# Softmax attention and linear attention on one core: the overflow guard moves from maxima of queries and keys to the row sums, and normalization and value copies move from VectorE to GpSimd

## The chip, the core and the metric

The kernel runs on one core of a Trainium2 chip. A core has a matrix engine (TensorE, "PE" in the profile), a vector engine (VectorE, "DVE"), an engine for activation functions (ScalarE, "ACT"), a general engine (GpSimd, "POOL") and a queue that issues transfers (SyncE, "SP"). PE writes its products into PSUM, eight banks of 128 x 512 float32; the others read PSUM or SBUF, and here POOL works on SBUF alone. The metric is the time of one execution on the device in microseconds (us).

## The reference

Two blocks of the same sizes are computed and set side by side in the output: A is linear attention, B is softmax attention. Each has its own input x (2048 x 512) and weights.

```python
B, S, D = 1, 2048, 512;  H = 32; Dh = 16
qkv = (x @ wqkv) -> q, k, v of (B, H, S, Dh)
# A: linear attention
phi = lambda t: jnp.where(t > 0, t + 1, jnp.exp(t)) + 1e-6
kv = jnp.einsum("bhsd,bhse->bhde", phi(k), v);  z = sum over s of phi(k)
o = (phi(q) @ kv) / (phi(q) @ z + 1e-6);  a = o @ wo
# B: softmax attention
p = softmax((q @ k.T) * Dh ** -0.5);  o = p @ v;  b = o @ wo
return jnp.concatenate([a, b], axis=-1)      # (1, 2048, 1024)
```

Almost all of the work is the 32 x 2048 x 2048 exponentials of block B.

## The kernel before

**Blocks and units.** The scores of B are made transposed, keys along the partitions, in blocks of 128 keys x 512 queries of one head: 32 heads x 4 query chunks x 16 key tiles = 2048 blocks. Heads are taken in four groups of eight (`Gp`). A unit (`unit(u)`, 32 of them) is one group, one chunk of 512 queries and either the even or the odd heads of the group: 4 heads x 16 key tiles = 64 blocks, whose products with the values accumulate in one PSUM bank `PVb`. The values `VV` have 17 columns for a head, the last of them ones, so that column 16 of the sum is the row sum of the softmax.

**Two ways to an exponential.** A block goes one of two ways. On the ACT way (`fill_act_cand`, L1022) ACT reads two or three score blocks from the PSUM regions `pS` and writes exp of them to `PT` in float16; each block then needs one product with the values. On the D way (`d_emit`, L923) a block lands in a bank of `pD` (or in the last bank of `pS`, which is "lent"), and DVE turns the scores into the bit patterns of float16 numbers with one multiply-and-add into int16 (`DI`): a straight line through the exponent. Three patterns shifted by a third of an octave each, weighted, approximate exp more closely; so up to three blocks of `DI` (1536 columns) are shifted twice (`shift_cand`, L1093) into `DJ`, on POOL as a rule, and PE multiplies `DI` and both `DJ` with three copies of the values, `VV` with k = 0, 1, 2, the last two weighted by `SW`. A D block costs ACT nothing, DVE one pass, POOL two shifts and PE three products.

**The other jobs.** `proj_job` projects queries and keys, copies them out of PSUM on DVE (L557, L563, L571) and then takes the largest absolute value of each 512 columns (L558 into `QMX`, L565 and L584 into `KMX`). `bound_job` (L595 to L601) and `flag_job` (L606, L607) turn these maxima into a bound on every score and leave the largest in `FLG`. `v4_job` projects four tiles of values: DVE copies them out of PSUM (L625) and makes the two weighted copies (L629), 32 of these in all. When a unit's sum is complete, `unit_done` transposes it on DVE into `OT` (L1241), takes reciprocals of the row sums (L1252), normalizes into `XN`, a part of the tile `OT` (L1246), and after each second unit transposes back into `ON` (L1256) for the output projection; `last_unit_done` (L1181 to L1189) does the last unit in halves. Block A's jobs (`akv_job` and the following ones) are spread over the run.

**What sets the order.** The program is planned when it is built: a loop keeps a clock for each engine, takes the candidate that can start first (ties by priority) and writes the instruction down. Each engine then runs its list in that order, with semaphore waits where data pass between engines. The durations in the code (0.62 for a reduction, `dp` and `dd` for a shift, the factors `PACE`) are the planner's, and are not measurements. How many blocks go the D way is no constant: `d_pick` (L869) gives a block to the D way whenever a bank is free, the planned backlog of DVE is at most `DBL` and that of POOL (`p_backlog`, L858) at most `PBL`, and a `DI` buffer is free. `shift_cand` gives a shift to DVE instead of POOL when POOL would end it more than `LM` = 5 us later.

**The guard.** A second, general program (`_general_softmax`) follows, for inputs whose scores could overflow the patterns. Every engine loads `FLG` into a register (L1480), 200 entries of the plan behind the instruction that writes it, and branches to the general program at its end only if the flag is above the threshold.

```python
d_pick:  if bi is None or u is None or dfree[bi] > at or d_backlog(at) > DBL or p_backlog(at) > PBL or lagging(at): return None
shift_cand:  dp, dd = 0.157 + w * 0.00095, 0.22 + w * 0.00047
             ln, st_, d_ = ("dve", sd, dd) if tp > td + LM else ("pool", sp, dp)
unit_done:   mul = f_op("dve", lambda e: e.tensor_tensor(xn[:, :, 16 * e_:16 * e_ + 16], o[:, :, 0:16], zr..., op=ALU.mult)
```

## Time and profile before

| What | Value |
|---|---|
| Runs, median (lowest to highest) | 701.72 us (701.65 to 701.93), 3 runs |
| Profiled execution, its own time | 701.74 us |
| Its span, first to last instruction | 700.0 us |
| Around the span | 1.74 us |
| Mean granted clock of PE | 0.999 |
| Busy: PE, DVE, ACT, POOL | 660.2, 619.5, 681.3, 577.1 us |

The profile is of one execution. "L923 DVE TENSOR_SCALAR DI<-pD 128x512 ... x431 | 285.5, 679 | 31.5 <-PE pD L821 26.5" reads: line 923 of the program, on DVE, writes DI from pD; 431 instructions that were busy for 285.5 us together, 679 ns each on average; ahead of them the engine sat idle for 31.5 us, of which 26.5 ended with a result of PE from line 821. Instructions of one engine overlap somewhat, so the busy time of a group can be less than its count times its mean. In a view of windows each row is a stretch of time and the columns are the busy time of each engine, with the number of its instructions. In a view of waits a row names who waited, for whom, how long in all, how often, and the longest. In a timeline a row begins with the start and the duration in us; the view of one line's instructions gives the shortest, median and longest duration in ns.

### The profile page before, as it was taken

To read this page: it belongs to the slowest core of one execution; us is meant where nothing else is said; L and a number is where in the kernel's file an instruction comes from. 1 tells how busy PE (TensorE), PEld (TensorE's weight loads), DVE (VectorE), ACT (ScalarE), POOL (GpSimd) and SP (SyncE) were. 2 spreads that over 40 slices of the span, in tenths; PEclk is the share of its full clock that TensorE was granted. 3 is DMA by queue.
4 is the path that set the end of the run, shared out by engine and by line. 5 is a ranking of instruction groups with operands and counts; after the bars stand their busy time and mean duration, and the time that the engine had idled before them with its cause. 6 is when DMAs were issued, how large, how long until landed. Compare 5 with 4: busy or idle time off the path is not lost.

```text
span 700.0 us, 19238 instructions
## 1 busy us (share of the span) xinstructions
PE 660.2 (94%) x8355; PEld 210.6 (30%) x8355; DVE 619.5 (88%) x994; ACT 681.3 (97%) x703; POOL 577.1 (82%) x409
## 2 busy tenths in 40 slices
PE   7999989999999999999999999999999999999996
PEld 4323333333333333332232233232322222322222
DVE  5999998898797989979998999999889999879993
ACT  5999999999999999999999999999999999999995
POOL 5689977776998889969967998889698898779983
PEclk9999999999999999999999999999999999999999
DMA  9300002211011000310012101110201100011001
GB/s 204 98 3 2 16 17 22 42 24 38 3 24 25 16 18 16 70 35 11 8 37 38 32 1 25 28 51 17 39 9 31 31 10 16 17 47 31 24 31 35
DMA packets 55418, 21.75 MB, mean 31 GB/s; under 512 B 45600, under 2 KB 55328, under 8 KB 55328
## 3 DMA queue, kind: packets, MB, share of 16 engines
q1 hardware_dynamic: 54272, 20.20, 13.2%
q8 instruction: 67, 1.10, 0.7%
q10 hardware_dynamic: 1056, 0.26, 0.2%
q14 instruction: 23, 0.19, 0.1%
HBM read 4.19 MB, written 4.19 MB: 12 GB/s over the span
## 4 chain that ended last, share of the span: by engine, by line
ACT 74%; DVE 16%; PE 7%; SPq 1%; issue 1%; DMA 1%; ACTq 0%
ACT PT L1022 71%; DVE DI L923 8%; PE pS L821 3%; PE pPV L1141 2%; ACT pD L641 2%; DVE VV L629 2%; DVE OT L1246 2%; PE pD L520 1%; SPq L371 1%; DVE VV L625 1%; DMA Wb<-in_B_wqkv_dram 1%; DVE OT L1241 1%; DVE KV L524 0%; PE pD L821 0%; DVE KV L640 0%
## 5 line engine op out<-in xcount | busy, mean ns | idle before, releaser
L1022 ACT ACTIVATE PT<-pS 128x1024 f16<-128x1024 f32 (+1 forms) x665 | 670.3, 1297 | 3.9 <-PE pS L821 1.6
L1093 POOL TENSOR_SCALAR DJ<-DI 128x1536 int16<-128x1536 int16 x384 | 569.7, 1485 | 110.3 <-DVE DI L923 86.5
L923 DVE TENSOR_SCALAR DI<-pD 128x512 int16<-128x512 f32 (+1 forms) x439 | 295.2, 689 | 32.0 <-PE pD L821 26.7
L821 PE MATMUL pS<-QT,KM 32*128 32x512 bf16 x1601 | 261.8, 384 | 24.2 <-ACT PT L1022 17.0
L1141 PE MATMUL pPV<-PT,VV 128*17 128x512 f16 x1446 | 244.1, 382 | 0.4 <-DVE VV L625 0.4
L1141 PE MATMUL pPV<-DJ,VV 128*17 128x512 f16 x1204 | 229.2, 382 | 0.4 <-DVE VV L629 0.4
L821 PE MATMUL pD<-QT,KM 32*128 32x512 bf16 x447 | 161.9, 384 | 1.9 <-DVE KV L524 0.9
L821 PEld LDWEIGHTS pS<-QT,KM 32*128 32x128 bf16 x1601 | 64.8, 91 | 274.4 <-ACT PT L1022 239.8
L1141 PE MATMUL pPV<-DI,VV 128*17 128x512 f16 x602 | 145.6, 382 | 0.3 <-DVE OT L1241 0.2
L923 DVE TENSOR_SCALAR DI<-pS 128x512 int16<-128x512 f32 x155 | 105.0, 678 | 4.2 <-PE pS L821 2.7
L1141 PEld LDWEIGHTS pPV<-PT,VV 128*17 128x17 bf16 x1446 | 50.2, 88 | 51.8 <-issue 44.8
L1141 PEld LDWEIGHTS pPV<-DJ,VV 128*17 128x17 bf16 x1204 | 48.0, 88 | 44.5 <-issue 33.8
L821 PEld LDWEIGHTS pD<-QT,KM 32*128 32x128 bf16 x447 | 38.4, 91 | 17.1 <-DVE DI L923 7.5
L1141 PEld LDWEIGHTS pPV<-DI,VV 128*17 128x17 bf16 x602 | 30.9, 88 | 20.8 <-issue 16.5
L520 PE MATMUL pD<-Wa,xTa 128*32 128x256 bf16 x896 | 34.6, 275 | 1.3 <-DVE DI L923 1.0
L1246 DVE TENSOR_TENSOR OT<-OT,ZR 128x256 bf16<-128x256 f32 x31 | 34.2, 1102 | 0.2
L520 PE MATMUL pD<-xTb,Wb 128*32 128x512 bf16 x400 | 29.4, 383 | 0.8 <-DVE DI L923 0.5
L629 DVE TENSOR_SCALAR VV<-VV 128x544 bf16<-128x544 bf16 x32 | 24.8, 789 | 0.0
L641 ACT ACTIVATE pD<-pD 128x512 f32<-128x512 f32 x30 | 23.6, 786 | 0.8 <-DVE KV L640 0.7
L520 PEld LDWEIGHTS pD<-Wa,xTa 128*32 128x32 bf16 x896 | 19.7, 96 | 14.4 <-issue 7.9
L1241 DVE STREAM_TRANSPOSE OT<-pPV 128x512 f32<-128x512 f32 x31 | 21.9, 707 | 0.4 <-PE pPV L1141 0.2
L520 PE MATMUL pD<-xTa,Wa 128*32 128x256 bf16 x512 | 19.8, 275 | 0.1
(98 smaller groups left out, 359.3 us busy)
## 6 DMA issues: line engine op xcount, KB each, us to landing
out_dram<-KV SPq DMA_DIRECT2D x32, 128.0 KB, 1.7
Wa<-in_A_wqkv_dram SPq DMA_DIRECT2D x3, 512.0 KB, 4.5
KM<-KR SPq DMA_DIRECT2D x96, 16.0 KB, 1.8
Wb<-in_B_wqkv_dram SPq DMA_DIRECT2D x2, 384.0 KB, 4.3
Wb<-in_B_wqkv_dram SPq DMA_DIRECT2D x1, 512.0 KB, 4.4
Wa<-in_A_wo_dram SPq DMA_DIRECT2D x1, 512.0 KB, 4.2
Wb<-in_B_wo_dram SPq DMA_DIRECT2D x1, 512.0 KB, 3.7
xTa<-in_A_x_dram SPq DMA_TRANSPOSE x24, 3.4
```

The lines of the kernel that those rows point to most:

```text
L371: sch.add(lane, lambda e: e.dma_start_transpose(dst[:, :, t0 * 128:(t0 + n) * 128], x[0][t0 * 128:(t0 + n) * 128, :]), writes=[(dname, t) ...
L520: ins = e.matmul(out[32 * g:32 * g + 32], lhsT=lhsT[:, 32 * g:32 * g + 32], rhs=rhs, start=start, stop=stop, tile_position=(0, 32 * g))
L625: st.append(("dve", 0.6, f_ev("dve", lambda e, bk: e.tensor_copy(VV[:, sl, 0, 4 * t4:4 * t4 + 4, :].rearrange("p t (h c) -> p t h c", c=17 ...
L629: st.append((lane, 0.4 if lane == "dve" else 0.71, f_op(lane, lambda e, k=k: e.tensor_scalar(vv(k), vv(0), SW[k], 0.0, op0=ALU.mult, op1=A ...
L641: ex = lambda bk: sch.add("act", lambda e: e.activation(x(bk), x(bk), ACTF.Exp), reads=[bk[3]], writes=[bk[3]])
L821: return e.matmul(dst, lhsT=KM[32 * g:32 * g + 32, Gp % 2, e_, j * 128:(j + 1) * 128], rhs=QT[32 * g:32 * g + 32, Gp % 2, c * 512:(c + 1) ...
L923: sch.add("dve", lambda e: e.tensor_scalar(DI[:, buf, i * 512:(i + n) * 512], f32v(DBANK[bi], 512 * n), ESC, EB, op0=ALU.mult, op1=ALU.add ...
L1022: sch.add("act", lambda e: e.activation(PT[:, row, c0:c0 + w], SCR[sl][:, 0:w], ACTF.Exp, scale=SC), reads=skeys(sl)[:len(bl)], writes=[(" ...
L1093: sch.add(ln, lambda e: e.tensor_scalar(J, I, 1.0, float(SH[k]), op0=ALU.mult, op1=ALU.add), reads=[("DI", buf, i) for i in range(n)], wri ...
L1141: sch.add("pe", lambda e, g=g, j=j, h=h, k=k, P=P, first=first, last_=last_: e.matmul(PVb[32 * g:32 * g + 17, 0:512], lhsT=VV[:, Gp % 2, k ...
L1241: sch.add("dve", lambda e: e.transpose(OT[:, 0, :], PVb[:, 0:512]), reads=[("PV", g) for g in range(4)], writes=[("OT", 0)])
L1246: mul = f_op("dve", lambda e: e.tensor_tensor(xn[:, :, 16 * e_:16 * e_ + 16], o[:, :, 0:16], zr.unsqueeze(2).broadcast_to([128, 16, 16]), ...
```

## The change

1. *The guard.* The maxima of queries and keys go (L558, L565, L584), and so does the bound made of them. The reciprocals of the row sums of all units, which were overwritten from unit to unit, are kept in `ZRA`. `sums_job` takes their largest and smallest when unit 30 is done (two reductions over 496 columns), `bound_job` adds the last unit's 16 columns and compares with 1/512 and 1/60000, `flag_job` brings the result to one number by a matmul into `PVb` and a reduction on DVE. These jobs are in a new list, `late`, with the lowest priority. PE, ACT, DVE and SP load the flag at the end of their lists, POOL behind its wait for the last stores.
2. *Clamped unsigned patterns.* Keys are stored multiplied by `ESC`, so the D way's first step is now an addition of `EB` and a minimum with `IMAX` into uint16; ACT's scale is divided by `ESC`.
3. *Normalization* of units 0 to 30 is issued on POOL (`XNP` = 1); `OT` and `XN` have one buffer each. *The weighted copies of the values* of groups 1 to 3 (24 of 32) are issued on POOL; those of group 0 stay on DVE.
4. *The planner.* POOL's planned shift becomes `POOLT(w)` = 0.284 + 0.00082 w with `PACE` 1.0 (before 0.157 + 0.00095 w with 1.01); a shift on DVE 0.40 + 0.0003 w (before 0.22 + 0.00047 w); `p_backlog` counts waiting shifts at `POOLT`; `PBL` goes from 6.5 to 7.5 and `SEED`, which jitters the due times of block A's jobs, from 14 to 18. On POOL a normalization has the priority 0.5, a shift 0.7 and a value copy 2 (the smaller goes first).
5. *Setting up.* The float32 identity, which only the general program uses, is no longer made at the start.

```diff
-    PBL = 6.5
+    PBL = 7.5
-    SEED = 14
+    SEED = 18
-    PACE = {"pe": 1.0, "act": 1.0, "dve": 1.03, "pool": 1.01, "dma": 1.0}
+    XNP = 1
+    VVP = 0
+    POOLT = lambda w: 0.284 + w * 0.00082
+    PACE = {"pe": 1.0, "act": 1.0, "dve": 1.03, "pool": 1.0, "dma": 1.0}
+    IMAX = 31743.0 - SH[2]
+    RMIN, RMAX = 512.0, 60000.0
...
-        OT = sb("OT", [128, 2, 512], F32)
-        XN = OT.bitcast(BF)[:, 1, :].rearrange("p (x n) -> p x n", n=512)
-        ZR = sb("ZR", [128, 2, 16], F32)
+        OT = sb("OT", [128, 1, 512], F32)
+        XN = sb("XN", [128, 1, 512], BF)
-        mk_ident(identf, "identf")
...
 proj_job
-                st.append(("dve", 0.62, f_op("dve", lambda e: e.tensor_reduce(QMX[:, i:i + 1], QT[:, r, cs], axis=AX.X, op=ALU.max,
-                                                                             apply_absolute_value=True), [("QT", r, sc)], [("QMX", i)])))
-                st.append(("dve", 1.2, f_op("dve", lambda e: e.tensor_reduce(KMX[:, i:i + 1], KM[:, r, :, cs], axis=AX.XY, op=ALU.max,
-            st.append(("dve", 0.62, reduce))
-            cp = f_ev("dve", lambda e, bk: e.tensor_copy(KR[:, kr, :], f32v(bk)), [], [("KR", kr)])
+            cp = f_ev("dve", lambda e, bk: e.tensor_scalar(KR[:, kr, :], f32v(bk), ESC, None, op0=ALU.mult), [], [("KR", kr)])
...
+        def red(dst, lo, hi, op):
+            return lambda e: e.tensor_reduce(ZRA[:, dst:dst + 1], ZRA[:, lo:hi], axis=AX.X, op=op)
+        ZL = 16 * (NU - 1)
+        def sums_job(**kw):
+            return Job([("dve", 0.6, f_op("dve", red(ZL + 16, 0, ZL, ALU.max), [("ZR", u) for u in range(NU - 1)], ["ZMX"])),
+                        ("dve", 0.6, f_op("dve", red(ZL - 1, 0, ZL, ALU.min), [("ZR", u) for u in range(NU - 1)], [("ZR", NU - 2)]))],
+                       [("zr", NU - 2)], [(1, "sums")], bank=False, **kw)
         def bound_job(**kw):
+                ("dve", 0.15, f_op("dve", red(ZL + 16, ZL, ZL + 17, ALU.max), ...
+                ("dve", 0.15, f_op("dve", red(ZL - 1, ZL - 1, ZL + 16, ALU.min), ...
+                ("dve", 0.12, f_op("dve", lambda e: e.tensor_scalar(BN1[:], ZRA[:, ZL + 16:ZL + 17], 1.0 / RMIN, None, op0=ALU.is_gt), ["ZMX"], ["BN1"])),
+                ("dve", 0.12, f_op("dve", lambda e: e.scalar_tensor_tensor(BN1[:], ZRA[:, ZL - 1:ZL], 1.0 / RMAX, BN1[:], op0=ALU.is_lt, op1=ALU.add),
         def flag_job(**kw):
+                ("pe", 0.3, f_op("pe", lambda e: e.matmul(PVb[0:1, 0:128], lhsT=BN1[:], rhs=BMk[:], start=True, stop=True), ["BN1", "BMk"], pvk)),
+                ("dve", 0.3, f_op("dve", lambda e: e.tensor_reduce(FLG, PVb[0:1, 0:128], axis=AX.X, op=ALU.max), pvk, ["FLG"]))],
...
-        def v4_job(t4, Gp, lane="dve", **kw):
+        def v4_job(t4, Gp, lane="pool", **kw):
-                st.append((lane, 0.4 if lane == "dve" else 0.71, f_op(lane, lambda e, k=k: e.tensor_scalar(
+                st.append((lane, 0.74 if lane == "dve" else 0.73, f_op(lane, lambda e, k=k: e.tensor_scalar(
...
 p_backlog
-            w += 1.13 * len(pend)
+            w += sum(POOLT(p_[3]) for p_ in pend)
-                    w += 1.13 * len(s_["items"])
+                    w += 2 * POOLT(512 * DG) / DG * len(s_["items"])
 d_emit
-                    sch.add("dve", lambda e: e.tensor_scalar(DI[:, buf, i * 512:(i + n) * 512], f32v(DBANK[bi], 512 * n),
-                                                             ESC, EB, op0=ALU.mult, op1=ALU.add),
+                    sch.add("dve", lambda e: e.tensor_scalar(DI.bitcast(U16)[:, buf, i * 512:(i + n) * 512], f32v(DBANK[bi], 512 * n),
+                                                             EB, IMAX, op0=ALU.add, op1=ALU.min),
 shift_cand
-            dp, dd = 0.157 + w * 0.00095, 0.22 + w * 0.00047
+            dp, dd = POOLT(w), 0.40 + w * 0.0003
-            return st_, 0, ln, d_, run, None, "f"
+            return st_, 0.7 if ln == "pool" else 0, ln, d_, run, None, "f"
...
 unit_done
-            mul = f_op("dve", lambda e: e.tensor_tensor(xn[:, :, 16 * e_:16 * e_ + 16], o[:, :, 0:16],
+            mul = f_op("pool" if XNP else "dve", lambda e: e.tensor_tensor(xn[:, :, 16 * e_:16 * e_ + 16], o[:, :, 0:16],
-                  ("dve", 0.68, norm)]
+                  ("pool", 0.82, norm) if XNP else ("dve", 0.96, norm)]
...
-        bjobs.append(bound_job(ready=0))
-        bjobs.append(flag_job(ready=0))
+        late = [sums_job(ready=0), bound_job(ready=0), flag_job(ready=0)]
...
-            sch.emit_queue(queue, e, sems, hook=(flag_op.idx + 200, hook))
-            with e.If(got[0] > THRESHOLD_BITS):
+            sch.emit_queue(queue, e, sems, hook=(flag_op.idx if queue == "pool" else len(sch.ops), hook))
+            with e.If(got[0] > FLAG_BITS):
```

More of the change, by code (lines that the diff above doesn't have):

```diff
@@ L135, in _general_softmax @@
     MBb = MB.bitcast(BF)
+    sch.add("dve", lambda e: e.memset(PVb[:], 0.0), writes=["PV"])
+    sch.add("pool", lambda e: e.memset(identf[:], 0.0), writes=["identf"])
+    sch.add("pool", lambda e: e.affine_select(out=identf[:], in_=identf[:], compare_op=ALU.not_equal, fill=1.0,
+                                              base=0, pattern=[[-1, 128]], channel_multiplier=1), reads=["identf"], writes=["identf"], force_signal=True)
     for Gp in range(4):
@@ L177, in _general_softmax @@
             sch.add("dve", lambda e: e.tensor_scalar(GM[:, 0, :], GM[:, 0, :], -1.0, None, op0=ALU.mult), reads=["GM"], writes=["GM"])
-            sch.add("pe", lambda e: e.transpose(MB[0:NT, 0:128], GM[:, 0, :], identf[:]), reads=["GM"], writes=["MB"])
+            sch.add("pe", lambda e: e.transpose(MB[0:NT, 0:128], GM[:, 0, :], identf[:]), reads=["GM", "identf"], writes=["MB"])
             sch.add("dve", lambda e: e.tensor_copy(GT, MB[0:NT, 0:128]), reads=["MB"], writes=["GT"])
@@ L331, in bass_concat_heads__linear_attn_block__softmax_full_mha__prompt_kernel @@
         PAR = sb("PAR", [128, 2], F32)
-        QMX = sb("QMX", [128, NGP * NC], F32)
-        KMX = sb("KMX", [128, NGP * NC], F32)
-        BND = sb("BND", [128, NGP], F32)
+        ZRA = sb("ZRA", [128, 16 * NU + 1], F32)
         BN1 = sb("BN1", [128, 1], F32)
-        FLG = sb("FLG", [1, 1], F32)
         NS, NA = len(ABL), sum(ABL)
@@ L407, in bass_concat_heads__linear_attn_block__softmax_full_mha__prompt_kernel @@
         mk_ident(identb, "identb")
[L408 to L409 removed]
+        sch.add("dve", lambda e: e.memset(DUM, 0.0), writes=["FLG"])
+        sch.add("act", lambda e: e.activation(DUM[:, 4:8], DUM[:, 0:4], ACTF.Exp), reads=["FLG"], writes=["FLG"])
         sch.add("dve", lambda e: e.memset(FZ[:], 0.0), writes=["FZ"])
@@ L604, in flag_job @@
         def flag_job(**kw):
+            pvk = [("PV", g) for g in range(4)]
             return Job([
-                ("pe", 0.3, f_pe(lambda e, bk: e.matmul(bk[0][0:1, bk[2]:bk[2] + 128], lhsT=BN1[:], rhs=BMk[:], start=True, stop=True), ["BN1", "BMk"])),
-                ("dve", 0.3, f_ev("dve", lambda e, bk: e.tensor_reduce(FLG[:], bk[0][0:1, bk[2]:bk[2] + 128], axis=AX.X, op=ALU.max), [], ["FLG"]))],
-                ["BN1"], [], **kw)
+                ("pe", 0.3, f_op("pe", lambda e: e.matmul(PVb[0:1, 0:128], lhsT=BN1[:], rhs=BMk[:], start=True, stop=True), ["BN1", "BMk"], pvk)),
+                ("dve", 0.3, f_op("dve", lambda e: e.tensor_reduce(FLG, PVb[0:1, 0:128], axis=AX.X, op=ALU.max), pvk, ["FLG"]))],
+                ["BN1"], [], bank=False, **kw)
@@ L632, in v4_job @@
             needs = ["WbV"] + [("xTb", t) for t in ts] + ([("pvdone", Gp - 2)] if Gp >= 2 else [])
-            return Job(st, needs, [(k, ("V", Gp, t, k)) for k in range(3) for t in ts], rel=0, **kw)
+            return Job(st, needs, [(k, ("V", Gp, t, k)) for k in range(3) for t in ts], rel=2 if VVP == 1 and lane == "dve" else 0, **kw)
         ectr = [0]
@@ L1291, in bass_concat_heads__linear_attn_block__softmax_full_mha__prompt_kernel @@
         urgent, urgent2, early, bjobs, ajobs = [], [], [], [], []
-        urgent2.append(Job([kmx], gives=[(0, ("KMX", 0))], bank=False, ready=30.0))
-        urgent2.append(Job([qmx], gives=[(0, ("QMX", 0))], bank=False, ready=30.0))
         for sc in range(1, NC):
@@ L1335, in job_cand @@
             bi = min((i for i in range(ND + 1) if dfree[i] is not None), key=lambda i: dfree[i], default=None)
-            for lst, pr in ((urgent, 0.5), (early, 2), (bjobs, 2.2), (urgent2, 2.3), (ajobs, 2.5)):
+            for lst, pr in ((urgent, 0.5), (early, 2), (bjobs, 2.2), (urgent2, 2.3), (ajobs, 2.5), (late, 2.7)):
                 for pos, j_ in enumerate(lst[:1] if lst is not urgent2 else lst[:8]):
@@ L1449, in bass_concat_heads__linear_attn_block__softmax_full_mha__prompt_kernel @@
                 TRACE.append((st, st + dur, eng, o[1]))
-        assert all(l_ == 0 for l_ in left) and pvu[0] == NU and not (urgent or urgent2 or early or bjobs or ajobs), \
+        assert all(l_ == 0 for l_ in left) and pvu[0] == NU and not (urgent or urgent2 or early or bjobs or ajobs or late), \
             (left, pvu, len(urgent), len(urgent2), len(early), len(bjobs), len(ajobs))
```

87 lines of the change are left out of this document (41 added, 46 removed).

## The prediction

> **What bounds the kernel now.** I read the page's busy times and chain first, then the groups by shape, the waits, the windows, and last the end of the span. The page, with the groups that count the blocks:
>
> ```profile
> span 700.0 us, 19238 instructions
> PE 660.2 (94%) x8355; PEld 210.6 (30%) x8355; DVE 619.5 (88%) x994; ACT 681.3 (97%) x703; POOL 577.1 (82%) x409
> ...
> ACT 74%; DVE 16%; PE 7%; SPq 1%; issue 1%; DMA 1%; ACTq 0%
> ...
> L1022 ACT ACTIVATE PT<-pS 128x1024 f16<-128x1024 f32 (+1 forms) x665 | 670.3, 1297 | 3.9 <-PE pS L821 1.6
> ...
> L1141 PE MATMUL pPV<-PT,VV 128*17 128x512 f16 x1446 | 244.1, 382 | 0.4 <-DVE VV L625 0.4
> ...
> L1141 PE MATMUL pPV<-DI,VV 128*17 128x512 f16 x602 | 145.6, 382 | 0.3 <-DVE OT L1241 0.2
> ```
>
> ACT is busy for 97% and idle for 3.9 us ahead of its exponentials. PE's 94% is not the bound, since PE waits for ACT, as this row of the waits says:
>
> ```profile
> PEld pS L821 <- ACT PT L1022: 239.8, 542, 0.9
> ```
>
> So the time is what ACT has to do. The products with PT count ACT's blocks, 1446, those with DI the D blocks, 602, together 2048. An ACT block costs 670.3 / 1446 = 0.4636 us of the span; everything in this change that is not at the two ends acts through the number of blocks that go the D way. What a D block costs the helpers, in the groups by shape:
>
> ```profile
> L923 DVE TENSOR_SCALAR DI<-pD 128x512 int16<-128x512 f32 x431 | 285.5, 679 | 31.5 <-PE pD L821 26.5 <-PE pS L821 2.3
> L923 DVE TENSOR_SCALAR DI<-pS 128x512 int16<-128x512 f32 x155 | 105.0, 678 | 4.2 <-PE pS L821 2.7 <-PE pD L821 0.7
> L923 DVE TENSOR_SCALAR DI<-pD 128x1024 int16<-128x1024 f32 x8 | 9.7, 1213 | 0.5 <-PE pD L821 0.2
> L1093 DVE TENSOR_SCALAR DJ<-DI 128x1536 int16<-128x1536 int16 x18 | 16.6, 923 | 0.0
> L1093 POOL TENSOR_SCALAR DJ<-DI 128x1536 int16<-128x1536 int16 x382 | 567.6, 1487 | 107.1 <-DVE DI L923 83.4
> L1093 POOL TENSOR_SCALAR DJ<-DI 128x1024 int16<-128x1024 int16 x2 | 2.1, 1046 | 3.2 <-DVE DI L923 3.1
> ```
>
> DVE: (285.5 + 105.0 + 9.7) / 602 = 0.665 us a block. Two shifts for three blocks: 2/3 x 1.487 = 0.991 us a block on POOL, or 2/3 x 0.923 = 0.615 on DVE. A D block is thus 1.656 us of helpers' time, 1.280 if DVE shifts it.
>
> **The change part by part.** What leaves DVE, and the rows that price what it gets:
>
> ```profile
> L558 DVE TENSOR_REDUCE QMX<-QT 128x1 f32<-128x512 bf16 x16 | 10.7, 675 | 0.1
> L584 DVE TENSOR_REDUCE KMX<-KR 128x1 f32<-128x512 bf16 x12 | 8.0, 670 | 0.0
> L565 DVE TENSOR_REDUCE KMX<-KM 128x1 f32<-128x1024 bf16 x4 | 4.8, 1205 | 0.0
> L599 DVE SCALAR_TENSOR_TENSOR BND<-BND,KMX 128x4 f32<-128x4 f32 x1 | 1.4, 1379 | 0.0
> L601 DVE TENSOR_REDUCE BN<-BND 128x1 f32<-128x4 f32 x1 | 0.2, 157 | 0.0
> L1246 DVE TENSOR_TENSOR OT<-OT,ZR 128x256 bf16<-128x256 f32 x31 | 34.2, 1102 | 0.2
> L629 DVE TENSOR_SCALAR VV<-VV 128x544 bf16<-128x544 bf16 x32 | 24.8, 789 | 0.0
> ```
>
> The maxima: 10.7 + 8.0 + 4.8 = 23.5 us, and 1.4 us of the old bound (its other small reductions are matched by new ones). The new guard adds two reductions over 496 columns, 0.675 each by L558, two of 17 columns at 0.157 and two column compares of no more than that: 2.0 us. Normalization: 34.2. Copies of values: 24 of the 32, 24 x 0.789 = 18.9. DVE loses 23.5 + 1.4 - 2.0 + 34.2 + 18.9 = 76.0 us.
>
> The two moved operations are long on DVE because of something outside them: the view of each one's instructions gives shortest, median and longest:
>
> ```profile
> L1246 DVE TENSOR_TENSOR OT<-OT,ZR x31: 415/1130/1728, 40.6 to 676.7; 128x256 bf16<-128x256 f32 x31
> ...
> L629 DVE TENSOR_SCALAR VV<-VV x32: 282/867/1555, 19.4 to 474.4; 128x544 bf16<-128x544 bf16 x32
> ```
>
> The same shape takes 415 ns or 1728. [...] I count the whole, since the rows are what DVE spent.
>
> What POOL gets is not in the trace of before in this form. A weighted copy reads one input of 544 columns: by the two POOL shifts, (1487 - 1046) / 512 = 0.86 ns a column, so 1046 - 480 x 0.86 = 0.633 us, an estimate; 24 x 0.633 = 15.2 us. A normalization reads two float32 inputs of 256 columns. Its ends are DVE's shortest, 0.415, and POOL's 1.487 for six times the columns. The nearest POOL rows are the float32 passes of the set-up:
>
> ```profile
> L403 POOL MEMSET identf<- 128x128 f32 x1 | 0.5, 504 | 0.0
> L404 POOL TENSOR_SCALAR_AFFINE_SELECT identf<-identf 128x128 f32<-128x128 f32 x1 | 0.3, 293 | 0.1
> L422 POOL TENSOR_SCALAR_AFFINE_SELECT BMk<-BMk 128x128 f32<-128x128 f32 x1 | 0.3, 339 | 0.1
> ```
>
> Twice 0.339 is 0.68 for 256 columns with one input; I take 0.8 for two: 31 x 0.8 = 24.8 us. POOL gets 40.0 and loses the identity's 0.504 + 0.293 = 0.8, so +39.2. The ends are 31 x 0.415 + 24 x 0.282 = 19.6 and 31 x 1.487 + 24 x 1.046 = 71.2. [...]
>
> The new waits: on POOL a normalization waits for DVE's reciprocal, with shifts queued behind it and PE's products of DJ behind those; on DVE the transposes into OT (once a unit, 32 units in 700 us, so each 22 us) and ON wait for POOL. `PVb` is free after the first transpose as before, so PE doesn't wait for POOL here. The copies of values are needed only by the next group's products, tens of us later. I cost these waits at zero; if POOL were late by more than a unit, DVE's transpose and then PE would stall.
>
> The clamp keeps two arithmetic steps from PSUM into 16 bits, so I leave L923 at 0.679. The ends are other passes of 512 columns out of PSUM, and 602 x (0.742 - 0.679) = 38 us would be the worst:
>
> ```profile
> L563 DVE TENSOR_SCALAR KM<-pD,PAR 128x512 bf16<-128x512 f32 x6 | 4.5, 742 | 0.7 <-PE pD L520 0.7
> L557 DVE CAST QT<-pS 128x512 bf16<-128x512 f32 x4 | 2.7, 672 | 0.0
> ```
>
> The scaled keys and ACT's other factor change no count and no shape: zero.
>
> How many blocks follow? DVE and POOL are busy for 619.5 + 577.1 = 1196.6 us, 1.709 of the span. I hold that share: at 602 blocks the new work is 1196.6 - 76.0 + 39.2 = 1159.8, which leaves 36.8 us. Each block more costs 1.656 and shortens the span by 0.4636, which takes 0.793 of room: 36.8 / 2.449 = 15 blocks, or 36.8 / 2.073 = 18 with DVE shifting; I take 16. That the load may pass from POOL to DVE is the planner's rule (a shift goes to DVE when POOL would be over 5 us later), and a fuller POOL calls it more often than 18 times. A second term is POOL's waiting:
>
> ```profile
> POOL DJ L1093 <- DVE DI L923: 86.5, 67, 5.0
> ```
>
> DVE has 76.0 of 619.5 less to do, 12%, and the early stretch has the most of it (all four long key maxima). I let a sixth of this wait go, 15 us, or 15 / 2.449 = 6 blocks; the ends are none and all of it (35 blocks). Together 22 blocks, 624 instead of 602: 22 x 0.4636 = 10.2 us. The stretches of 100 us show room for it:
>
> ```profile
> 100.00:200.00 100.00, 96.47 (x1338) 32.44 (x1336) 85.43 (x141) 99.70 (x105) 76.69 (x53) 1.00 0.14 26
> 200.00:300.00 100.00, 95.17 (x1309) 32.84 (x1309) 90.64 (x147) 99.30 (x107) 89.89 (x61) 1.00 0.14 31
> ```
>
> POOL (the fifth pair) reaches 89.89 in one and 76.69 in another. With 577.1 + 39.2 and about 12 shifts more it would have 634 of 690, 92%: just above its best stretch, the point on which the forecast leans.
>
> **The two ends.** The guard now ends last. The flag loads of before, the gap they made on ACT, and DVE and ACT at the end:
>
> ```profile
> L1480 POOLq TENSOR_LOAD <-FLG x1: 495/495/495, 560.9 to 560.9; - x1
> ...
> 562.38 4.62 ACT L1022 ACTIVATE PT<-pS 128x1024 f16<-128x1024 f32 x4 [0.53 <-issue]
> ...
> 694.16 0.45 DVE L1189 STREAM_TRANSPOSE ON<-OT 128x256 bf16<-128x256 bf16 x1
> 695.11 0.69 DVE L524 CAST KV<-pS 128x512 bf16<-128x512 f32 x1 [0.51 <-PE pS L520]
> 695.33 0.60 ACT L524 ACTIVATE KV<-pS 128x512 bf16<-128x512 f32 x1 [0.35 <-PE pS L520]
> ```
>
> The four small bound instructions, 4 x 0.157 = 0.63 us, fit into DVE's 0.51 us gap but for 0.12, and the CAST then ends at 695.92, still ahead of ACT's 695.93. Behind them wait that CAST, the flag's matmul and its reduction; all of it runs while the last stores land. If that cover were gone it would cost 1 to 2 us. POOL loads the flag only behind its wait for the stores: +0.5 us. ACT's gap of 0.53 in the middle goes. I take zero for both, between -0.5 and +1.5.
>
> The sum is made against the profiled execution's own 701.74 us (span 700.0), 0.02 above the median of the runs: 701.74 - 10.2 = 691.5.
>
> **The rivals.** *More than that (674 us).* All the time freed on DVE becomes D blocks that DVE shifts itself: 76.0 / 1.280 = 59 blocks, 27.5 us. For it speaks that the planner can give DVE shifts; against it that POOL comes first and only a lag of 5 us sends a shift over.
>
> *The D share stays (701.8 us).* Blocks are limited by free banks and by PE, not by the helpers: DVE waits 26.5 us for scores ahead of L923. Then the freed time is idle time, and only the ends move, by about 0.1.
>
> *POOL becomes the bound: slower (711 us).* POOL's work goes ahead of the shifts in its queue, it waits there for DVE's reciprocals, and its 110 us of idle time ahead of shifts (107.1 + 3.2) can't be filled. If POOL's busy time can't rise at all, 39.2 / 1.487 = 26 shifts fall away, 39 blocks or +18.3 us; half of that gives 711. It decides from the point where POOL can't get past 616 us in the same span without DVE taking the rest. For it speaks that POOL's 82% over the span lies well below its best stretch, against it that the idle time is DVE's doing. [...]
>
> That the new guard sends the run into the general program has 0.01; for the reference's inputs (weights and x near 0.05) the scores are near zero, so each of a row's 2048 terms is near 1 and its sum near 2048, between the limits 512 and 60000.
>
> **How the numbers follow.** Forecast 0.61 (its own range 685 to 699), more 0.10, share stays 0.12, POOL the bound 0.16. The range reaches from 679 to 704: low, 12.5 us below by POOL's cheap end (20 us, 8 blocks, 3.8 us) and 19 blocks of POOL's waiting (8.7 us); high, 12.5 above, where POOL's dear end (+5.9), no waiting regained (+2.8) and a part of the clamp's 38 us (up to +7.2) add to more than that. The rest, about 0.2, lies outside on both sides. Within 0.2% is 1.4 us, about what these runs can tell. Faster: 0.61 + 0.10 and 0.04 of the third; same 0.07; slower 0.18.
>
> **What would show it.** Right: products with DI near 624 and with PT near 1424, POOL busy near 630, DVE below 580, L1246 on POOL near 0.8 us, more than 18 shifts on DVE, POOL's wait for DVE below 86.5. Wrong: fewer than 602 products with DI, L923 above 0.70, ACT idle ahead of L1022 by more than 10 us, or the span's end more than 2 us later behind the last ACT copy than now.

## The result and the profile after

The changed kernel takes 691.09 us (median of 4 runs, 690.96 to 692.18), the kernel before beside it 701.83; the ratio is 0.9843, interval 0.9825 to 0.986. The prediction was 691.5, so the time is right to 0.4 us. Two of its terms were not, and that they cancelled is luck. The page after (busy times; the chain of waits by engine; ACT's exponentials; then the counts of blocks), whose profiled execution took 691.10 us:

```profile
span 689.4 us, 19282 instructions
PE 652.7 (95%) x8384; PEld 208.4 (30%) x8384; DVE 569.4 (83%) x929; ACT 673.1 (98%) x696; POOL 613.8 (89%) x464
...
ACT 93%; PE 4%; DVE 2%; DMA 1%; issue 0%
...
L1031 ACT ACTIVATE PT<-pS 128x1024 f16<-128x1024 f32 (+1 forms) x658 | 664.9, 1371 | 1.9 <-PE pS L830 1.7
...
L1150 PE MATMUL pPV<-PT,VV 128*17 128x512 f16 x1432 | 246.1, 382 | 0.5 <-ACT PT L1031 0.3
...
L1150 PE MATMUL pPV<-DI,VV 128*17 128x512 f16 x616 | 147.2, 382 | 0.5 <-DVE OT L1251 0.5
```

616 D blocks instead of 602, not 624. Fourteen blocks are 14 x 0.4636 = 6.5 us, but the span is 10.6 shorter. Where the rest is, the timelines of ACT say: the first and the last run of exponentials, before and then after, and behind them the last copy after; the last copy before, 695.33 to 695.93, is among the lines of the prediction (start, duration):

```profile
9.66 1.94 ACT L1022 ACTIVATE PT<-pS 128x1024 f16<-128x1024 f32 x2 [0.58 <-PE pD L821]
...
687.46 3.77 ACT L1022 ACTIVATE PT<-pS 128x1536 f16<-128x1536 f32 x3
```

```profile
9.07 4.71 ACT L1031 ACTIVATE PT<-pS 128x1024 f16<-128x1024 f32 x5 [0.66 <-PE pS L830]
...
676.47 3.17 ACT L1031 ACTIVATE PT<-pS 128x1024 f16<-128x1024 f32 x3
...
683.95 0.60 ACT L531 ACTIVATE KV<-pS 128x512 bf16<-128x512 f32 x1 [0.51 <-PE pS L527]
```

| Part of the span (us) | before | after | difference |
|---|---|---|---|
| up to the first exponential | 9.66 | 9.07 | -0.6 |
| first exponential to the end of the last | 681.57 | 670.57 | -11.0 |
| of it ACT blocks x 0.4636 | 670.4 | 663.9 | -6.5 |
| of it the rest | 11.2 | 6.7 | -4.5 |
| end of the last exponential to the end of the last copy | 4.70 | 4.91 | +0.2 |
| end of the last copy to the end of the span | 4.07 | 4.85 | +0.8 |

The rest, 4.5 us, is ACT waiting less between exponentials. It hardly shows as idle time (1.9 us ahead of L1031, 3.9 before): ACT's recorded instructions overlap (an exponential of two blocks is recorded with 1.299 us on average after the change, yet one ends every 0.916 us), and a short wait vanishes in the overlap.

The ends of ACT's records, taken one by one, measure it. Where nothing holds ACT up, an exponential of two blocks ends 0.916 us behind the instruction before it, one of three blocks 1.343 us, an activation of block A 0.490 us (lower quartiles, the same before and after within 0.001 us). That is ACT's own time; what a record takes beyond it is a wait. Before, the stretch is 674.5 us of own time and 7.1 of waits, after it 668.0 and 2.5: 6.5 us are blocks and 4.5 are waits.

The chain of waits says who held ACT up. Before, it leaves ACT often for DVE, mostly for L923; DVE had 16% of the chain and has 2% now:

```profile
ACT PT L1022 71%; DVE DI L923 8%; PE pS L821 3%; PE pPV L1141 2%; ACT pD L641 2%; DVE VV L629 2%; DVE OT L1246 2%; PE pD L520 1%; SPq L371 1%; DVE VV L625 1%; DMA Wb<-in_B_wqkv_dram 1%; DVE OT L1241 1%; DVE KV L524 0%; PE pD L821 0%; DVE KV L640 0%
```

The moved work, in the groups by shape:

```profile
L1256 POOL TENSOR_TENSOR XN<-OT,ZRA 128x256 bf16<-128x256 f32 x31 | 19.3, 622 | 1.3
L638 POOL TENSOR_SCALAR VV<-VV 128x544 bf16<-128x544 bf16 x24 | 15.4, 647 | 0.9
```

```profile
L638 DVE TENSOR_SCALAR VV<-VV 128x544 bf16<-128x544 bf16 x8 | 3.0, 386 | 0.0
L1102 DVE TENSOR_SCALAR DJ<-DI 128x1536 int16<-128x1536 int16 x26 | 23.7, 913 | 0.0
L932 DVE TENSOR_SCALAR DI<-pD 128x512 uint16<-128x512 f32 x456 | 303.9, 682 | 61.3 <-PE pD L830 52.2 <-PE pS L830 6.2
```

And the waits that the prediction named, POOL's for DVE and DVE's for PE, after and, for the second, before:

```profile
DVE DI L932 <- PE pD L830: 55.1, 114, 1.6
POOL DJ L1102 <- DVE DI L932: 36.1, 32, 3.9
```

```profile
DVE DI L923 <- PE pD L821: 27.4, 55, 1.6
```

POOL waits 50 us less for DVE, DVE 28 us more for scores. Two of the windows after; POOL is the fifth pair, ACT the fourth:

```profile
100.00:200.00 100.00, 96.22 (x1352) 31.89 (x1345) 83.07 (x136) 100.00 (x105) 87.73 (x63) 1.00 0.11 23
200.00:300.00 100.00, 96.01 (x1317) 33.37 (x1317) 86.12 (x140) 100.00 (x106) 95.66 (x71) 1.00 0.16 31
```

POOL went past the 89.89 that was its best stretch before, and ACT, 99.70 and 99.30 there before, shows no gap.

One thing is needed to read the runs below. Executions of one kernel differ in the mean granted clock of PE, 0.975 to 1.000, and as a rule their times with it: the experiment "Without the general program" took 688.6 and 688.8 us at 1.000 and 691.1 twice at 0.994, 0.4 us for 0.001. In the traces a lower mean is a piece of 3.4 us, or a few of them, at half the clock. I give medians as measured and, as "at 0.999", the median after taking 0.4 us for each 0.001 below 0.999 from every run. The kernel before is then 701.3 to 701.7 in every comparison; the changed kernel 690.4. The runs of the kernel before by themselves give 0.35 us for 0.001, and those of some kernels below follow no such line, so a time at 0.999 is good to about 1 us. ACT's waits are therefore given without those that overlap such a piece or begin within 3 us behind it ("at the full clock"): 7.1 us before, 1.5 after. One run, of the experiment "Another seed", lay more than 1.5% above the fastest of its kernel and is left out.

### The profile page after: what moved, and what is told of

It is laid out like the page before. It is cut to its first block, busy times and chain, and to the rows that moved or that the text cites. A ratio compares the mean times of both kernels' runs of the same rounds, so it can differ in the third digit from the quotient of the medians.

```text
span 689.4 us, 19282 instructions
## 1 busy us (share of the span) xinstructions
PE 652.7 (95%) x8384; PEld 208.4 (30%) x8384; DVE 569.4 (83%) x929; ACT 673.1 (98%) x696; POOL 613.8 (89%) x464
## 4 chain that ended last, share of the span: by engine, by line
ACT 93%; PE 4%; DVE 2%; DMA 1%; issue 0%
ACT PT L1031 91%; ACT pD L650 2%; PE pS L830 1%; PE pD L527 1%; DVE DI L932 1%; DMA xTb<-in_B_x_dram 1%; PE pPV L1150 1%; ACT pS L650 1%; DVE DJ L1102 0%; PE pS L527 0%; PE pD L621 0%; PE pD L830 0%; DVE ON L1199 0%; DVE OT L1191 0%; DVE KV L531 0%
## 5 line engine op out<-in xcount | busy, mean ns | idle before, releaser
L1031 ACT ACTIVATE PT<-pS 128x1024 f16<-128x1024 f32 (+1 forms) x658 | 664.9, 1371 | 1.9 <-PE pS L830 1.7
L1102 POOL TENSOR_SCALAR DJ<-DI 128x1536 int16<-128x1536 int16 (+1 forms) x386 | 573.8, 1488 | 60.7 <-DVE DI L932 36.1
L932 DVE TENSOR_SCALAR DI<-pD 128x512 uint16<-128x512 f32 (+1 forms) x466 | 316.1, 694 | 63.0 <-PE pD L830 53.7
L830 PE MATMUL pS<-QT,KM 32*128 32x512 bf16 x1572 | 257.0, 385 | 26.1 <-ACT PT L1031 19.4
L830 PE MATMUL pD<-QT,KM 32*128 32x512 bf16 x476 | 169.7, 385 | 0.6 <-DVE DI L932 0.4
L932 DVE TENSOR_SCALAR DI<-pS 128x512 uint16<-128x512 f32 x140 | 95.2, 680 | 6.4 <-PE pS L830 3.8
L1102 DVE TENSOR_SCALAR DJ<-DI 128x1536 int16<-128x1536 int16 x26 | 23.7, 913 | 0.0
L1256 POOL TENSOR_TENSOR XN<-OT,ZRA 128x256 bf16<-128x256 f32 x31 | 19.3, 622 | 1.3
L531 DVE CAST KV<-pD 128x512 bf16<-128x512 f32 x25 | 17.1, 682 | 3.6 <-PE pD L527 3.4
L650 ACT ACTIVATE pD<-pD 128x512 f32<-128x512 f32 x23 | 19.7, 857 | 0.0
```

Source lines behind the costliest of these rows:

```text
L531: return lambda e, bk: (e.tensor_copy(out_fn(), in_fn(bk)) if lane == "dve" else e.activation(out_fn(), in_fn(bk), ACTF.Copy))
L650: ex = lambda bk: sch.add("act", lambda e: e.activation(x(bk), x(bk), ACTF.Exp), reads=[bk[3]], writes=[bk[3]])
L830: return e.matmul(dst, lhsT=KM[32 * g:32 * g + 32, Gp % 2, e_, j * 128:(j + 1) * 128], rhs=QT[32 * g:32 * g + 32, Gp % 2, c * 512:(c + 1) ...
L932: sch.add("dve", lambda e: e.tensor_scalar(DI.bitcast(U16)[:, buf, i * 512:(i + n) * 512], f32v(DBANK[bi], 512 * n), EB, IMAX, op0=ALU.add ...
L1031: sch.add("act", lambda e: e.activation(PT[:, row, c0:c0 + w], SCR[sl][:, 0:w], ACTF.Exp, scale=SC / ESC), reads=skeys(sl)[:len(bl)], writ ...
L1102: sch.add(ln, lambda e: e.tensor_scalar(J, I, 1.0, float(SH[k]), op0=ALU.mult, op1=ALU.add), reads=[("DI", buf, i) for i in range(n)], wri ...
```

## The experiments

A part that is undone makes the planner write another order, and how many D blocks come of it depends also on luck (the experiment "Another seed"). So in the first three experiments, in the two whose titles end in "planned with the durations that its trace shows" and "planned too short", and in "All three back on DVE" the seed is the one of 0 to 29 whose plan ends first, as 14 is for the kernel before and 18 for the changed one. Over these 30 seeds the plans of the kernel before have 581 to 602 D blocks, median 590, and those of the changed kernel 590 to 616, median 605. So some 15 blocks are the change's and not a lucky seed's.

**Normalization back on DVE.**

```diff
-    XNP = 1
-    SEED = 18
+    XNP = 0
+    SEED = 14
```

> The changed kernel with the 31 normalizations back on DVE (planned there with 0.96 us, as the change provides); the plan then has 606 D blocks instead of 616. Theory A, only the number of blocks counts (0.4636 us each): 691.1 + 10 x 0.4636 = 695.7 us, and the chain of waits stays with ACT (DVE about 2%). Theory B, besides the blocks each operation on DVE that waits for POOL's instruction to end makes ACT wait a little (the part of the gain that the blocks don't explain, 4.5 us over the 55 moved operations, 0.08 us each): 2.5 us more, 698.3 us, and DVE's share of the chain is clearly above 2%, with the normalization's line in it.

699.57 us, ratio to before 0.9952 (0.993 to 0.9975); at 0.999 696.0. DVE has 3% of the chain. The normalization on DVE:

```profile
L1256 DVE TENSOR_TENSOR XN<-OT,ZRA 128x256 bf16<-128x256 f32 x31 | 27.2, 876 | 0.3
```

By the blocks it is 690.4 + 10 x 0.4636 = 695.0; the measured 696.0 is 1.0 above, against 2.5 that B asked for. The chain is as A has it, and ACT's waits at the full clock are 1.7 us against 1.5: B's waits aren't there. On POOL the operation takes 0.622 us, less than the 0.876 on DVE beside a busy POOL.

**Copies of values back on DVE.**

```diff
-        def v4_job(t4, Gp, lane="pool", **kw):
+        def v4_job(t4, Gp, lane="dve", **kw):
-    SEED = 18
+    SEED = 12
```

> The changed kernel with all weighted copies of the values on DVE (24 more there), 615 D blocks. Theory A: 691.1 + 0.5 = 691.6 us. Theory B: 24 x 0.08 = 2 us more, 693.6 us, with the copies' line in the chain of waits. The copies on DVE should take 0.7 to 0.9 us on average, against 0.386 for the eight that are there now.

693.75 us, 0.9875 (0.9844 to 0.9905); at 0.999 691.9. The blocks give 690.4 + 0.5 = 690.9, so by the time this is halfway between A and B. ACT's waits at the full clock are 1.7 us against 1.5, which speaks for A. DVE has 3% of the chain. The copies are long again, as expected:

```profile
L638 DVE TENSOR_SCALAR VV<-VV 128x544 bf16<-128x544 bf16 x32 | 23.7, 749 | 0.1
```

**Maxima back.** The reductions of the kernel before are put back after the copies of queries and keys; the guard doesn't use them.

```diff
+                st.append(("dve", 0.62, f_op("dve", lambda e: e.tensor_reduce(QMX[:, i:i + 1], QT[:, r, cs], axis=AX.X, op=ALU.max,
+                                                                             apply_absolute_value=True), [("QT", r, sc)], [("QMX", i)])))
...
+            st.append(("dve", 0.62, reduce))
-    SEED = 18
+    SEED = 27
```

> The changed kernel with the maxima of queries and keys taken on DVE again (32 reductions, their results unused), 610 D blocks. These reductions have one input and took between 658 and 687 ns before, so they don't wait for POOL. Theories A and B both: 691.1 + 6 x 0.4636 = 693.9 us, and DVE's share of the chain stays about 2%. If DVE's load itself makes ACT wait, it is 695 us or more.

699.13 us, 0.9946 (0.9928 to 0.9965); at 0.999 695.1, where the blocks give 693.2. (Of these reductions L558's took 658 to 687 ns before, on average 675 where POOL was running at their start and 676 where it wasn't, L584's 642 to 676; the four of L565 have twice the columns and took 1202 to 1208.) DVE's share of the chain is 1%. So the load itself may cost a little, 1.9 us beyond the blocks, without DVE coming into the chain; in the profile, whose execution was the fastest of the five, ACT's waits at the full clock are 2.2 us, 0.7 above the changed kernel's.

**As many D blocks as before.**

```diff
+            if sum(sum(c_) for c_ in dcnt) >= (2048 - sum(left)) * 602 / 2048.0 + 3:
+                return None
             ch = choose(u, 1, used, True)
```

> The changed kernel in which the planner may give only as many blocks to the D way as the kernel before had, spread evenly; it has 600. If the time goes by the number of ACT blocks: 691.1 + 16 x 0.4636 = 698.5 us, and about 4 us of the gain stays beside the blocks. If the gain came from elsewhere (less waiting, whatever the split), it stays near 692 us. If freeing the helpers of 16 blocks gives ACT fewer waits as well: 696 to 698.

700.38 us, 0.9965 (0.9951 to 0.998); at 0.999 696.2. Sixteen blocks fewer cost 5.8 us where the count says 7.4. That is the size of the third case, but little of it is fewer waits: ACT's own time grows by 6.4 us instead of 7.4, since more of its exponentials have three blocks (147 instead of 117), and its waits at the full clock fall from 1.5 to 1.1 us. With 600 blocks this is still 5 us faster than the kernel before at the same clock (701.3) with 602: that part of the gain isn't the blocks.

**Another seed.**

```diff
-    SEED = 18
+    SEED = 5
```

> The changed kernel with SEED 5 in place of 18, nothing else: only the jitter of block A's due times is another, and 592 D blocks come of it. By the blocks: 691.1 + 24 x 0.4636 = 702.2 us, as slow as the kernel before, so that the choice of the seed is worth as much as the whole change. If the seed's share is smaller than the count says, 695 us or less.

709.13 us, 1.0063 (1.0034 to 1.0092): slower than the kernel before. Its nine runs go from 703.4 to 711.8 with the clock from 0.992 to 0.975; at 0.999 they are 700.6 to 702.3, median 701.7, against 701.5 by the blocks. A seed with few D blocks (5 has the plan that ends last of the 30) undoes the whole change, and its clock falls on top. Two windows of it:

```profile
300.00:400.00 100.00, 93.83 (x1173) 28.51 (x1167) 75.45 (x120) 99.67 (x105) 74.37 (x53) 1.00 0.12 28
...
500.00:600.00 100.00, 93.43 (x1133) 27.45 (x1130) 79.48 (x127) 97.00 (x97) 79.52 (x57) 0.94 0.09 23
```

Where the clock (third from the end) is 0.94, ACT, the fourth pair, loses 2.7 us of 100. Of ACT's waits, 10.2 us in all, 8.3 lie in or just behind the pieces at half the clock.

**The kernel before with another seed.**

```diff
-    SEED = 14
+    SEED = 18
```

> The kernel before with SEED 18 in place of 14, nothing else: 584 D blocks instead of 602. By the blocks 701.8 + 18 x 0.4636 = 710.1 us. If it is within 2 us of 701.8, the number of blocks isn't what sets the time.

714.93 us, 1.0179 (1.0155 to 1.0203); at 0.999 711.4. Slower by 9.7 us at equal clock, by the blocks 8.3. The chain keeps DVE's share, so that share doesn't belong to the seed, and ACT's waits at the full clock are 7.9 us:

```profile
ACT 74%; DVE 14%; PE 9%; SPq 1%; DMA 1%; issue 1%; DVEq 0%
```

**The kernel before, planned with the durations that its trace shows.**

```diff
-                  ("dve", 0.68, norm)]
+                  ("dve", 1.07, norm)]
-                st.append((lane, 0.4 if lane == "dve" else 0.71, f_op(lane, lambda e, k=k: e.tensor_scalar(
+                st.append((lane, 0.77 if lane == "dve" else 0.71, f_op(lane, lambda e, k=k: e.tensor_scalar(
-            dp, dd = 0.157 + w * 0.00095, 0.22 + w * 0.00047
+            dp, dd = 0.157 + w * 0.00095, 0.40 + w * 0.0003
-    SEED = 14
+    SEED = 16
```

> The kernel before with the same work on the same engines, but the planner told the durations on DVE that the trace of before shows (normalization 1.10 us instead of 0.70, weighted copies 0.79 instead of 0.41, a shift on DVE 0.86 instead of 0.94), and SEED 16; 594 D blocks instead of 602. By the blocks alone 701.8 + 8 x 0.4636 = 705.5 us. Theory B (the waits for POOL themselves hold up ACT) says 705.5, with DVE still about 16% of the chain of waits. Theory C (ACT waited because the plan reckoned too short with these operations, so that the order of PE's work was wrong by what they took longer) says that the 4.5 us of hidden waits go: 701 us, with DVE's share of the chain falling to some 2 to 5%.

705.93 us, 1.0049 (1.0029 to 1.0069); at 0.999 702.9. With 8 blocks fewer it is 1.2 us slower than the kernel before at that clock (701.7) instead of 3.7. By the time alone that is between B and C. The chain is C's:

```profile
ACT 89%; PE 5%; DVE 3%; DMA 1%; SPq 1%; issue 0%; ACTq 0%
```

The operations are all on DVE still and take about as long there as before (normalization 1.015 us, copies 0.866, on average; 1.102 and 0.789 before), and yet most of DVE's part of the chain is gone. ACT's waits at the full clock are 4.2 us instead of 7.1; another seed alone moved them by 0.8. The profiled executions of this kernel and of the one with seed 18 both have the clock 0.993; the rest of ACT's stretch is 10.5 us here and 15.2 there.

**Normalization on DVE, planned too short.**

```diff
-    XNP = 1
+    XNP = 0
-                  ("pool", 0.82, norm) if XNP else ("dve", 0.96, norm)]
+                  ("pool", 0.82, norm) if XNP else ("dve", 0.68, norm)]
-    SEED = 18
+    SEED = 29
```

> The changed kernel with the normalizations on DVE, as in the first experiment, but planned with 0.70 us as in the kernel before instead of 0.99; 611 D blocks against 606 there. By the blocks it is 5 x 0.4636 = 2.3 us faster than that experiment. Theory B: the same hidden waits in both, so 2.3 us faster. Theory C (a plan that reckons too short makes ACT wait): the hidden waits are larger here, and the difference shrinks to nothing or turns round; DVE's share of the chain of waits is larger here than there.

695.1 us, 0.989 (0.987 to 0.9911); at 0.999 692.9, where the blocks give 692.7. It is 3.1 us faster than the first experiment at equal clock; B said 2.3, C nothing. DVE has 3% of the chain in both:

```profile
ACT 91%; PE 4%; DVE 3%; DMA 1%; issue 0%
...
L1256 DVE TENSOR_TENSOR XN<-OT,ZRA 128x256 bf16<-128x256 f32 x31 | 27.5, 886 | 0.1
```

So the normalization planned at 0.70 us while it takes 0.886 doesn't bring the waits back; at the full clock they are 1.4 us. C in the form in which I stated it falls for this one operation when it is planned 0.19 us short; in the kernel before it was 0.40 short (0.70 against 1.102), and that was not run. What the experiment before this one corrected besides was not taken apart: the copies, planned at about half, and the shift on DVE, which had been planned a little long (0.94 us, where it took 0.923).

**The early flag load.** POOL loads the flag ahead of its wait for the stores.

```diff
+        sch.add("pool", lambda e: e.memset(EARLYT[:], 0.0), writes=["EARLY"])
         sch.add("pool", lambda e: None, extra_deps=list(last.values()), name="final")
```

> The changed kernel in which POOL loads the flag ahead of its wait for the last stores instead of behind it (one small memset of a tile of its own stands between). If the load behind the stores is what lengthened the stretch from ACT's last copy to the end of the span from 4.07 to 4.85 us, this stretch goes back to about 4.1 and the time to 690.4 us. If the guard's chain itself or the branch sets the end, both stay, 691.1.

691.91 us, 0.985 (0.9831 to 0.9869): no gain over the changed kernel. The loads of the flag after the change, and here:

```profile
L1487 ACTq TENSOR_LOAD <-FLG x1: 466/466/466, 684.6 to 684.6; - x1
...
L1487 POOLq TENSOR_LOAD <-FLG x1: 498/498/498, 686.7 to 686.7; - x1
```

```profile
L1489 ACTq TENSOR_LOAD <-FLG x1: 464/464/464, 686.2 to 686.2; - x1
L1489 POOLq TENSOR_LOAD <-FLG x1: 482/482/482, 686.2 to 686.2; - x1
```

POOL does load it at once, at 686.2, but from the last copy (686.10) to the end (691.2) it is 5.1 us all the same. The load behind the stores isn't what ends last. What does is PE's branch over the general program, whose record runs to 689.0 in the changed kernel, where POOL's load ends at 687.2. In the kernel before it ran to 698.9, and POOL's branch, behind the stores, began after it, at 699.3. The branches of PE and POOL after, and of PE before:

```profile
L1489 PEldq COMPARE_BRANCH  x1: 3606/3606/3606, 685.4 to 685.4; - x1
L1489 POOLq COMPARE_BRANCH  x1: 53/53/53, 687.3 to 687.3; - x1
```

```profile
L1482 PEldq COMPARE_BRANCH  x1: 4211/4211/4211, 694.7 to 694.7; - x1
```

**Without the general program** and without the branch over it (the fallback for large scores is left out; the flag is still made and loaded):

```diff
-            with e.If(got[0] > FLAG_BITS):
...
-                gsch.emit_queue(queue, e, gsems)
```

> The changed kernel without the general program and without the branch over it (this leaves the fallback for large scores out); every engine still loads the flag as in the changed kernel. The early load on POOL didn't shorten the end of the span: from ACT's last copy to the end it was 4.07 us before, 4.85 after, 5.10 with the early load. If what follows the load on the other engines (the branch over the general program) sets the end, then without it the end comes with the stores and POOL's load: about 3 us from the last copy, 689.3 us in all. If the stores themselves set it, it stays near 4.85 and 691.1.

689.95 us, 0.9824 (0.9798 to 0.9849); at 0.999 689.1, 1.3 below the changed kernel. From the last copy it is 689.3 - 686.20 = 3.1 us to the end, as expected of the branch:

```profile
685.60 0.60 ACT L531 ACTIVATE KV<-pS 128x512 bf16<-128x512 f32 x1 [0.51 <-PE pS L527]
```

So the branch sets the end of the span, in these profiles 1.75 us past what the stores and POOL's load take.

**All three back on DVE,** with the planner's constants of the change; the maxima are put back as in the third experiment:

```diff
-    XNP = 1
+    XNP = 0
-        def v4_job(t4, Gp, lane="pool", **kw):
+        def v4_job(t4, Gp, lane="dve", **kw):
...
-    SEED = 18
+    SEED = 26
```

> The changed kernel with all three on DVE again (normalizations, weighted copies, and the maxima, their results unused), with the planner's constants of the change and SEED 26; 600 D blocks. Take ACT's stretch from its first to its last exponential less 0.4636 us for each ACT block: this rest was 11.2 us before and 6.7 after. By the blocks alone 691.1 + 16 x 0.4636 = 698.5 us and a rest of about 6.7. If DVE's heavier load itself makes ACT wait (whatever the plan knows), the rest comes near 10.5 and the time is 702 us. If it was the planner's durations, which are nearer to the trace here than in the kernel before, the rest stays at 6.7 to 7.5 and DVE's share of the chain of waits at about 3%.

702.87 us, 1.0007 (0.9995 to 1.0019): the kernel before again, and as measured the 702 us of the first case. But its clock is lower, 0.988 to 0.994. At 0.999 it is 699.1; the blocks give 697.8, so 1.3 us are beyond them. These ten runs don't follow the clock (at 0.999 they spread from 697.8 to 701.8), so the time alone doesn't decide. DVE has 3% of the chain, not 16, though POOL waits for it 72.4 us, against 86.5 before and 36.1 after:

```profile
ACT 90%; PE 4%; DVE 3%; DMA 1%; issue 0%
```

```profile
POOL DJ L1116 <- DVE DI L946: 72.4, 55, 8.1
```

The rest of ACT's stretch is 10.0 us in a profile at 0.991. Of ACT's waits, 5.7 us, 2.9 are those of one stretch of 10.2 us at half the clock near the start; at the full clock there are 2.7, against 7.1 in the kernel before and 1.5 after the change. So with the planning of the change the same load on DVE costs about 1.3 us beyond the blocks, not the 4.6 of the kernel before.

**A faster version.** More backlog allowed for POOL, and others of the planner's values; POOL's early load is in it as well, and the seed is none of 0 to 29:

```diff
-    PBL = 7.5
-    SEED = 18
-    DLEAD = 0.8
-    ALAG = 30.0
+    PBL = 9.0
+    SEED = 185
+    DLEAD = 1.2
+    ALAG = 60.0
```

> The changed kernel with the early flag load and other values of the planner: SEED 185, PBL 9.0, DLEAD 1.2, ALAG 60; 627 D blocks instead of 616. By the blocks 691.1 - 11 x 0.4636 = 686.0 us, with the flag's 0.7 us 685.3. If POOL, which has then some 640 of 685 us of work, becomes the bound, PE waits for DJ and the time stays at 689 us or above.

688.06 us, 0.9795 (0.9776 to 0.9813), faster than both; at 0.999 685.8, where the blocks give 685.3. POOL isn't the bound: it is less busy than after the change, since DVE does 39 shifts instead of 26.

```profile
PE 655.6 (95%) x8403; PEld 207.5 (30%) x8403; DVE 581.7 (84%) x936; ACT 669.4 (97%) x708; POOL 608.5 (88%) x460
...
L1102 DVE TENSOR_SCALAR DJ<-DI 128x1536 int16<-128x1536 int16 x39 | 33.9, 869 | 0.0
```

**All of them on one line.** The times at 0.999 beside 690.4 + 0.4636 (616 - n), and from one profile each ACT's own time and its waits at the full clock, all in us:

| Kernel | D blocks n | at 0.999 | by the blocks | difference | ACT's own time | its waits |
|---|---|---|---|---|---|---|
| faster version | 627 | 685.8 | 685.3 | +0.5 | 664.1 | 1.2 |
| after | 616 | 690.4 | 690.4 | 0 | 668.0 | 1.5 |
| copies on DVE | 615 | 691.9 | 690.9 | +1.0 | 669.0 | 1.7 |
| normalization on DVE, planned short | 611 | 692.9 | 692.7 | +0.2 | 670.6 | 1.4 |
| maxima back | 610 | 695.1 | 693.2 | +1.9 | 671.0 | 2.2 |
| normalization on DVE | 606 | 696.0 | 695.0 | +1.0 | 673.5 | 1.7 |
| capped | 600 | 696.2 | 697.8 | -1.6 | 674.4 | 1.1 |
| all three on DVE | 600 | 699.1 | 697.8 | +1.3 | 675.6 | 2.7 |
| seed 5 | 592 | 701.7 | 701.5 | +0.2 | 678.5 | 1.9 |
| before, durations of the trace | 594 | 702.9 | 700.6 | +2.3 | 678.4 | 4.2 |
| before | 602 | 701.5 | 696.9 | +4.6 | 674.5 | 7.1 |
| before, seed 18 | 584 | 711.4 | 705.2 | +6.2 | 682.1 | 7.9 |

From 592 to 627 blocks the nine kernels with the change's planning fall by 16 us, 0.454 us a block; ACT's own time for a block is 0.458 us in an exponential of two blocks and 0.448 in one of three. Around the line they scatter from -1.6 to +1.9 us. The kernels with the old durations lie 4.6 and 6.2 us above it. When the durations on DVE are corrected, and the seed chosen anew, 2.3 are left, which by the time alone is near the scatter. ACT's waits are the clearer sign: 7.1 and 7.9 us with the old planning, 4.2 with the durations on DVE corrected, 1.1 to 2.7 in all nine kernels with the planning of the change, whichever engine has the moved operations. With the blocks it is the other way round. Over the 30 seeds the median plan has 605 D blocks after the change, 603 with the copies back on DVE, 601 with the maxima, 596 with the normalization, 588 with all three, and 590 in the kernel before. So the blocks come from the work that left DVE, the waits from the planning.

## Why the prediction was right, step by step

*That the time follows ACT's blocks, 0.4636 us each*: shown, over a range of 35 blocks, for plans of one kind. The price is a little high: it was taken from records that overlap and hold the waits of the kernel before.

*What leaves DVE, 76.0 us*: the maxima's groups, 23.5, and the normalization, 34.2, are gone, and the copies went from 24.8 to 3.0, so 21.8 instead of 18.9. The copies that stay cost 0.386 us on average, not 0.789; five of the eight begin with POOL idle and take 0.282 to 0.302 us. The prediction counted the moved rows whole, as what DVE spent, and put their length down to something outside the operations. The trace of before shows what: all 31 normalizations begin while a shift runs on POOL, and 30 of them, 0.465 to 1.728 us long, end 0.27 us behind the end of that shift (the other, which began 0.03 us ahead of that end, took 0.415). Of the 32 copies 24 begin so, take 0.310 to 1.555 us and end 0.15 us behind the shift; the eight that begin with POOL idle take 0.282 to 0.291. DVE's busy time fell by only 50.1. 14 blocks and 8 shifts more came to it (11.1 + 7.1 us), so its durations added up fell by 61.3; the other 11 us are overlap, since the records of DVE overlap each other by 60.2 us before and 48.9 after.

*What POOL gets, 39.2 us*: 19.3 for the normalization (24.8 predicted, 0.622 us each against 0.8) and 15.4 for the copies (15.2). POOL is not the slower of the two for the normalization here: beside a POOL that is busy for 79 to 87% of the span the operation takes 0.855 to 1.102 us on DVE on average, though 0.415 at its shortest.

*The clamp at nothing*: right, 682 ns against 679.

*That DVE and POOL keep their common share of the span, hence 15 blocks*: right in this case. (569.4 + 613.8) / 689.4 = 1.716 against 1.709, and 14 blocks came. The share is no constant, though: it is 1.618 in the changed kernel with seed 5 and 1.644 in the kernel before with seed 18. It holds, with 1.69 to 1.73, for the best plans of 30 seeds, whichever engine has the moved work.

*The 6 blocks from POOL's waiting*: this is the term that failed. POOL's wait fell by 50 us instead of 15, and not one block came of it beyond the 14; DVE now waits for PE's scores instead (55.1 us). The helpers' slack moved from POOL to DVE; it didn't turn into work. So the term of 22 blocks, 10.2 us, measured 14 blocks, 6.5 us.

*That everything between the ends acts through the number of blocks*: wrong, and this made good the error before, by luck: the prediction has no term for it. ACT's waits between its exponentials fell by 4.5 us. The prediction read "ACT 97%" and 3.9 us idle as a full engine, and passed over the 16% of DVE in the same chain. That share was the sign: ACT waited in pieces too short to be seen beside its overlapping records. The capped kernel shows the gain without the blocks, 5 us. It comes from the planning more than from the moved operations: with all three on DVE and the planning of the change, ACT's waits at the full clock rise only from 1.5 to 2.7 us, while they were 7.1 in the kernel before. Correcting the durations on DVE alone takes the kernel before to 4.2. What brings the rest stays open; POOL's planned shifts, the limits on the backlogs, the priorities and the buffers were not taken apart. Nor was it settled which of the durations on DVE matters; a normalization planned 0.19 us short doesn't bring the waits back.

*The two ends at zero*: the guard's four small instructions were hidden, as said: the CAST starts 0.50 us behind the last transpose after the change (0.50 before).

```profile
682.78 0.45 DVE L1199 STREAM_TRANSPOSE ON<-XN 128x256 bf16<-128x256 bf16 x1
683.15 0.21 DVE L588 TENSOR_REDUCE ZRA<-ZRA 128x1 f32<-128x17 f32 x2
683.31 0.15 DVE L601 TENSOR_SCALAR BN<-ZRA 128x1 f32<-128x1 f32 x1
683.50 0.16 DVE L602 SCALAR_TENSOR_TENSOR BN<-ZRA,BN 128x1 f32<-128x1 f32 x1
683.73 0.69 DVE L531 CAST KV<-pS 128x512 bf16<-128x512 f32 x1
```

The +0.5 us of the load was put on POOL, behind the stores. It was +0.8 in this profile and 0.8 to 1.5 in those of the nine other kernels that load the flag at the end, with the branch behind it, and it sits on the engines whose branch ends later than the stores. From the branch to the next record ACT, DVE and PE take 3.3 to 3.7 us after the change, SP and POOL 0.2. Without the branch the span ends 1.75 us sooner behind the last copy; what that time goes to no run shows.

*The rivals.* "POOL becomes the bound" fell: POOL is busy for 89% of the span and for 95.66 us of its best hundred, with 386 shifts instead of 384 and the new work besides. "The D share stays" fell with 616. "More than that" didn't come: only 8 shifts more went to DVE.
